# Folding w_phi into the key and query weights in blocks of six whole heads, with Wq transposed out of DRAM, Wv loaded in halves and a second order of the steps

## The chip, the cores and the metric

The kernel runs on one core of one Trainium2 chip. The metric is device time in microseconds (us) of one execution; three executions of the kernel before gave 236.93, 237.06 and 239.13 us, so the median is 237.06 us. Below, TensorE is PE, VectorE is DVE, ScalarE is ACT, GpSimd is POOL, and SyncE, which here only issues DMAs, is SP.

## The reference

There are 2048 tokens of 640 numbers in bf16, 32 heads of 20, and a second layer of 1728 hidden units.

```
qkv  = layernorm(x) @ wqkv                     # (2048, 3*640): q, k, v
pq   = einsum("bhsd,hdf->bhsf", q, w_phi)      # w_phi: (32, 20, 20), one small matrix per head
pk   = einsum("bhsd,hdf->bhsf", k, w_phi)
phi_q = concat(softmax(pq), softmax(-pq))      # 40 features per head
phi_k = concat(softmax(pk), softmax(-pk))
kv   = einsum("bhsf,bhsd->bhfd", phi_k, v);  z = sum over s of phi_k
o    = (phi_q @ kv) / (phi_q @ z + 1e-6)
h    = x + o @ wo
out  = h + silu(layernorm(h) @ w1) @ w2
```

## The kernel before

**Folding.** q and k are used only through w_phi. So the kernel multiplies the weights first: Wfk = Wk @ blockdiag(w_phi) and Wfq = Wq @ blockdiag(w_phi), both 640 x 640, and projects the tokens with these. PE contracts over partitions, so Wk and Wq have to be transposed to be the stationary operand. A row chunk `ce` holds 128 of the 640 input rows; there are C = 5 of them.

- Wk is loaded in five chunks (L168) and each is transposed on PE in five 128 x 128 pieces (`wk0` to `wk4`, L306), copied out of PSUM by DVE or ACT (`wke`, L323) into WTk, folded (`fk`, six matmuls into a pair of banks, L333) and copied into Wfk (`fk0e` and so on, L342).
- Wq is loaded whole (800 KB, L180). When it has landed, five SBUF-to-SBUF DMA transposes (`wq0` to `wq4`, L325) write WTq; `fq` and `fq0e` fold it as `fk` does.
- The pieces of 128 columns cut through heads (128 is not a multiple of 20). Each piece is therefore multiplied with a slab `phi` of 240 columns that overlaps its neighbours, and the overlaps are summed in PSUM: per chunk six matmuls of 80, 140 and 240 columns, 920 in all. `phi` is built by DVE out of w_phi and a 0/1 mask `own` (`phi_a`, `phi_b`, L292); POOL makes the mask.

**Tokens.** They are in T = 16 tiles of 128. For each tile t of X: `st` (L373, L374: mean and variance, DVE), `rs` (1/std, ACT or POOL), `xn` (normalised tile, L389, DVE 0.4 us or POOL 2.5 us), `xt` (transpose; on PE for the first four tiles, L396, by a DMA for the others, L418), `x` (copy into XnT for the first four, L416). Then `K` and `V` (ten matmuls of 320 columns each, L429), `ex` (exponentials, ACT, L461), `su` (sums, DVE, L465), `rk` (ACT), `sc` (scaling, DVE, L478), `ve` (values to SBUF, ACT, L482) and `kv` (eleven matmuls of 63 columns or fewer that add to the key-value matrix in PSUM banks 6 and 7, L497). The queries (`Q`, `qe`, `qs`, `qr`, `qt`), attention (`D`, `E`), the output projection (`G`, `ga`), the second layernorm (`ls`, `lr`, `hn`, `ht`) and the second layer (`u`, `s`, `lt`, `d`, `oa`, `out`) follow, overlapping.

**What sets the order.** Everything after the first loads is emitted by hand: ORDER is one list of step names, and each engine runs its own steps in the order of that list. ON says which engine does a step that several could do. The weights and X are loaded from SP's queue before the list starts: X tile 0, the five chunks of Wk, X tile 1, all of Wv, X tiles 2 and 3, all of Wq, X tiles 4 to 7, X tiles 8 to 15. The steps `load0` to `load11` bring wo, w1 and w2 later. `warm0` to `warm21` are matmuls on constants.

**Banks.** PSUM banks 0 to 5 are three pairs handed out in turn (`ps_pair`): a step that takes a pair waits until whoever read its previous content is done. Through the K and V stage each `wk` pair, `xt`, `fk`, `fq`, `K` and `V` takes the next pair; V of tile 0 alone is put into banks 6 and 7. There are four EK buffers and four VP buffers.

Of the kernel before, what the change touches and what calls it, by code (L numbers as in the profile page):

```python
# [30 lines left out]
ex15 su14 load8 Q2 ve14 qr1 rk14 V15 su15 qe2 qt1 Q3 sc12 ve15 sc13 rk15 Q4 qe3 sc14 sc15 kv12 qe4
kv13 qs2 kv14 kv15 Q5 qr2 Q6 qe5 bd1 qt2 bd0 Q7 qe6 qs3 qe7 halves D0 Q8 E00 E01 D1 qe8 qs4 Q9 ot0
load9 E10 Q10 qe9 load10 E11 Q11 qr3 qe10 qt3 D2 qe11 G00 E20 G01 ga00 ot1 Q12 ga01 E21 ls0 Q13 ot2
qe12 lr0 Q14 qe13 hn0 ht0 G10 qe14 D3 ga10 G11 load11 Q15 ga11 E30 E31 G20 qe15 ls1 u0.L ot3 u0.0
s0.L ga20 lr1 lt0 u0.4 s0.0 hn1 qr4 G21 ht1 s0.4 u0.8 ga21 ls2 u0.12 s0.8 G30 s0.12 lr2 G31 ga30 d00
hn2 ga31 ht2 ls3 qt4 u1.L qs5 lr3 u1.0 s1.L d01 hn3 s1.0 oa00 ht3 qr5 lt1 u1.4 oa01 qs6 qt5 u1.8
s1.4 qr6 u1.12 s1.8 out0 u2.L D4 s1.12 u2.0 qs7 s2.L lt2 d10 s2.0 qs8 qt6 E40 u2.2 E41 d11 s2.2 oa10
ot4 qr7 D5 oa11 u2.4 qs9 u2.6 s2.4 E50 u2.8 s2.6 E51 ot5 u2.10 s2.8 u2.12 qt7 s2.10 D6 s2.12 G40 E60
G41 E61 d20 ga40 ot6 ga41 ls4 out1 lr4 hn4 ht4 G50 G51 d21 ga50 oa20 ga51 ls5 d30 lr5 hn5 d31 qr8
ht5 oa21 oa30 G60 oa31 G61 ga60 qs10 D7 u4.L u4.0 s4.L lt4 E70 u4.2 s4.0 ga61 E71 u4.4 s4.2 qr9 ot7  # L40
u4.6 s4.4 ls6 qt8 u4.8 s4.6 lr6 out2 u4.10 qt9 s4.8 hn6 qr10 u4.12 s4.10 qt10 s4.12 out3 ht6 G70 G71
ga70 d40 ga71 ls7 lr7 D8 oa40 d41 E80 hn7 qs11 ht7 d50 E81 qr11 d51 oa41 qt11 oa50 qs12 u6.L u6.0
ot8 s6.L oa51 u6.2 s6.0 lt6 D9 s6.2 out4 u6.4 E90 E91 u6.6 s6.4 qr12 ot9 u6.8 s6.6 qs13 qt12 G80
s6.8 u6.10 u6.12 s6.10 D10 s6.12 G81 E100 G90 ga80 ga81 d60 ga90 ls8 E101 G91 lr8 d61 ot10 hn8 oa60
ga91 out5 ls9 ht8 d70 qr13 lr9 hn9 d71 oa61 ht9 out6 qt13 G100 G101 ga100 oa70 D11 oa71 u8.L u8.0
ga101 s8.L E110 u8.2 E111 s8.0 qs14 ot11 u8.4 s8.2 lt8 u8.6 qr14 s8.4 u8.8 ls10 qt14 s8.6 u8.10 lr10
s8.8 out7 hn10 u8.12 s8.10 qs15 ht10 s8.12 G110 G111 ga110 D12 d80 E120 ga111 E121 d81 ls11 ot12
oa80 lr11 d90 hn11 oa81 ht11 qr15 d91 oa90 G120 G121 ga120 oa91 u10.L D13 s10.L u10.0 lt10 E130 E131
u10.2 s10.0 ga121 ot13 ls12 u10.4 s10.2 lr12 u10.6 s10.4 hn12 u10.8 s10.6 ht12 u10.10 s10.8 out8
out9 qt15 u10.12 s10.10 D14 s10.12 G130 G131 ga130 d100 ga131 ls13 E140 lr13 d101 hn13 oa100 ht13  # L50
d110 oa101 E141 ot14 d111 oa110 out10 u12.L u12.0 s12.L D15 s12.0 u12.2 E150 oa111 G140 s12.2 E151
u12.4 ga140 ot15 u12.6 s12.4 out11 lt12 G141 s12.6 u12.8 ga141 ls14 u12.10 s12.8 lr14 G150 s12.10
hn14 u12.12 ga150 ht14 G151 s12.12 d120 ga151 ls15 lr15 d121 oa120 hn15 ht15 d130 oa121 out12 u14.L
oa130 u14.0 s14.L lt14 u14.2 s14.0 u14.4 s14.2 u14.6 s14.4 u14.8 s14.6 u14.10 s14.8 u14.12 s14.10
d131 s14.12 d140 oa131 out13 d141 oa140 d150 oa141 out14 d151 oa150 out150 d152 oa151 out151 oa152
out152
# [4 lines left out]
def kernel(  # L61
# [70 lines left out]
    def ps_half_bf16():  # L132
# [13 lines left out]
        phi_b="DVE", rs0="ACT", phi_a="DVE", xn0="DVE", wke0="ACT", wke1="ACT", wke2="DVE", wke3="ACT",  # L146
        x0="DVE", fk1e="ACT", fk2e="ACT", wke4="DVE", rs1="POOL", fk3e="DVE", fk4e="ACT", xn1="DVE",
        fk0e="ACT", rs2="ACT", x1="ACT", xn2="DVE", rs3="ACT", xn3="DVE", x2="DVE", rs4="POOL", xn4="DVE",
        rs5="POOL", xn5="POOL", x3="ACT", fq0e="ACT", rs6="POOL", fq1e="ACT", rs7="ACT", xn6="DVE", xn7="POOL",
        rs8="ACT", xn8="POOL", rs9="ACT", xn9="POOL", fq2e="ACT", fq3e="ACT", rs10="ACT", xn10="POOL",  # L150
        fq4e="ACT", rs11="POOL", xn11="POOL", rs12="ACT", rs13="POOL", xn12="DVE", xn13="POOL", rs14="ACT",
        xn14="POOL", rs15="ACT", xn15="POOL",
    )


    Wk = early.tile([P, C, D], BF16, name="Wk")
    Wq = early.tile([P, C, D], BF16, name="Wq")
    WPH = early.tile([P, C, DH], BF16, name="WPH")
# [8 lines left out]
    def load_wk(queue, a, b):  # L167
        queue.dma_start(Wk[:, a:b], wqkv_v[:, a:b, D : 2 * D])  # L168

    nc.scalar.dma_start(WPH[:], A_w_phi.rearrange("h d f -> (h d) f").rearrange("(r p) f -> p r f", p=P))  # L170
    load_x(0, 1)
    load_wk(nc.sync, 0, 1)
    load_wk(nc.sync, 1, 2)
    load_wk(nc.sync, 2, 3)
    load_wk(nc.sync, 3, 4)
    load_wk(nc.sync, 4, 5)
    load_x(1, 2)
    nc.sync.dma_start(Wv[:], wqkv_v[:, :, 2 * D : 3 * D])  # L178
    load_x(2, 4)
    nc.sync.dma_start(Wq[:], wqkv_v[:, :, 0:D])  # L180
    load_x(4, 8)
    load_x(8, 16)
# [25 lines left out]
    NV = 4  # L208
# [33 lines left out]
    def ones(i):  # L242
        nc.gpsimd.memset(VP[i][:, :, DH:HV], 1.0)
        nc.gpsimd.memset(EK[i][:, H * HF :], 0.0)

    assert NV == NE
# [14 lines left out]
    for side in range(2):  # L261
# [20 lines left out]
    nc.gpsimd.affine_select(
        out=own[:], in_=own[:], compare_op=ALU.is_ge, fill=0.0,
        base=DH - 1, pattern=[[-8, NB], [DH, 8]], channel_multiplier=-1,
    )
    nc.gpsimd.memset(phi[:, :, 8 * DH : BW], 0.0)
    ps_of = {}

    def phi_own(b):

        a, n = 3 * b, 3 - b
        engines[on(f"phi_{'ab'[b]}", "DVE")].tensor_tensor(  # L292
            phi[:, a : a + n, 0 : 8 * DH].rearrange("p r (h f) -> p r h f", f=DH),
            WPH[:, a : a + n].unsqueeze(2).to_broadcast([P, n, 8, DH]),
            own[:, a : a + n].unsqueeze(3).to_broadcast([P, n, 8, DH]), op=ALU.mult,
        )
# [5 lines left out]
    WTq = early.tile([P, C, NB, P], BF16, name="WTq")  # L302

    def transposed(W, ce, pt):
        for r in range(NB):
            nc.tensor.transpose(pt[:, r, :], W[:, ce, r * P : (r + 1) * P], ident[:])  # L306

    def wk(k, ce):
        if k == 4:

            pt = kv_bf[:, 1]
        else:
            if k % 2 == 0:
                ps_of["wk", "pair", k // 2] = ps_pair_bf16()
            pt = ps_of["wk", "pair", k // 2][:, k % 2]
        ps_of["wk", ce] = pt
        transposed(Wk, ce, pt)

    WKS = (0, 1, 2, 3, 4)
    for k, ce in enumerate(WKS):  # L320
        eng = on(f"wke{ce}", ("ACT", "DVE")[k % 2])
        add(f"wk{ce}", lambda k=k, ce=ce: wk(k, ce))
        add(f"wke{ce}", lambda ce=ce, e=copies[eng]: e(WTk[:, ce], ps_of.pop(("wk", ce))[:, 0:NB]))  # L323
    for ce in range(C):
# [523 lines left out]
```

## Time and profile before

| what | value |
|---|---|
| median of three executions | 237.06 us |
| span of the profiled execution, first to last instruction | 235.7 us |
| granted TensorE clock over the span | 1.000 |
| PE busy | 230.5 us, 98% |
| DVE / ACT / POOL busy | 170.0 / 107.8 / 46.7 us |
| PE busy from 30 to 200 us | 170.0 of 170.0 us |
| ten matmuls of 320 columns (a K or a V), start to start | 1.36 us |
| five 128 x 128 transposes on PE, start to start | 0.28 us |
| six matmuls of one fold, start to start | 0.40 us |
| eleven matmuls of one kv step, start to start | 0.34 us |
| copy of 640 columns out of PSUM, one instruction | ACT 0.69 us, DVE 0.44 to 0.49 us from bf16, 0.81 us from float32 |
| Wk chunk, issue to landing | 2.6 to 3.9 us |
| Wq, 800 KB, issue to landing | 8.3 us |
| X tiles 8 to 15, 1280 KB, issue to landing | 13.4 us |
| DMA transpose into XnT, issue to landing | 2.4 to 6.7 us, median 3.3 us |

The span is less than the measured time by 1.36 us against the median. A time read on one engine is turned into an effect on the end only where that engine, or whoever waits for it, has nothing else to do meanwhile. Durations of neighbouring instructions on one engine overlap by about 0.1 us (PE's by 0.16 us), so start-to-start distances are used for sums.

### The profile page before, as it was taken

The page shows a single profiled execution, that of the slowest core. Times are in us where ns is not written, and L with a number is a line of the kernel's source. Part 1 is how long each engine was busy: PE and PEld are TensorE (multiplying, and loading weights), DVE is VectorE, ACT ScalarE, POOL GpSimd, SP SyncE. Part 2 cuts the span into 40 slices and gives each one's busy share as a digit, 9 for nine tenths or more (in the row PEclk, how much of TensorE's full clock was granted, in tenths as well). Part 3 has the DMA queues.
Part 4 walks back from the last instruction along what each step waited for, and adds up shares of the span by engine and source line. Part 5 has one row for each costly group of instructions (what it writes and reads, how often), then busy time and mean ns, then how long its engine had stood idle before and what let it go on. Part 6 is the DMA issues. An engine that isn't in the chain of part 4 may idle for free.

```text
span 235.7 us, 5600 instructions
## 1 busy us (share of the span) xinstructions
PE 230.5 (98%) x2256; PEld 181.4 (77%) x2256; DVE 170.0 (72%) x355; ACT 107.8 (46%) x230; POOL 46.7 (20%) x80
## 2 busy tenths in 40 slices
PE   8899999999999999999999999999999999999995
PEld 6677777777777779798877878877877977877874
DVE  4699999899999758899669787696885544463021
ACT  3788997997888777231401501400510420421500
POOL 3117778990000011200020110011001100010000
PEclk9999999999999999999999999999999999999999
DMA  6996858499452842864431695617445193222001
GB/s 167 328 389 129 103 141 170 128 202 281 101 108 64 209 88 52 107 143 92 89 86 28 139 165 116 123 32 136 85 108 55 33 147 83 31 61 61 3 29 56
DMA packets 66697, 27.50 MB, mean 117 GB/s; under 512 B 58992, under 2 KB 65648, under 8 KB 66544
## 3 DMA queue, kind: packets, MB, share of 16 engines
q1 hardware_dynamic: 66016, 27.13, 53.2%
q8 instruction: 17, 0.28, 0.5%
q10 hardware_dynamic: 656, 0.03, 0.2%
q14 instruction: 8, 0.07, 0.1%
HBM read 10.43 MB, written 2.62 MB: 55 GB/s over the span
## 4 chain that ended last, share of the span: by engine, by line
PE 90%; DMA 6%; SPq 2%; issue 0%; DVE 0%; DVEq 0%
PE banks L733 24%; PE banks L771 24%; PE banks L429 15%; PE banks L444 9%; PE banks L643 9%; DMA Wq<-in_A_wqkv_dram 4%; DMA WTq<-Wq 3%; PE banks L497 2%; PE banks L610 2%; PE banks L774 2%; PE banks L744 1%; PE banks L333 1%; SPq L168 1%; SPq L165 1%; SPq L178 0%
## 5 line engine op out<-in xcount | busy, mean ns | idle before, releaser
L771 PE MATMUL banks<-w_sb,shT 128*128 128x320 bf16 (+2 forms) x429 | 61.3, 295 | 0.0
L733 PE MATMUL banks<-HnT,w_sb 128*128 128x256 bf16 (+1 forms) x585 | 60.0, 261 | 0.0
L733 PEld LDWEIGHTS <-w_sb 128*128 128x128 bf16 x585 | 51.3, 98 | 5.4
L771 PEld LDWEIGHTS <-shT 128*128 128x128 bf16 x429 | 41.1, 98 | 15.0
L753 ACT ACTIVATE shT<-banks 128x512 bf16<-128x512 f32 (+2 forms) x57 | 31.4, 559 | 36.0 <-PE banks L733 34.6
L429 PEld LDWEIGHTS <-XnT 128*128 128x128 bf16 x320 | 30.3, 98 | 12.0 <-issue 1.1
L382 POOL TENSOR_SCALAR rs<-mv 128x1 f32<-128x1 f32 x22 | 5.0, 227 | 159.9 <-DVE mv L374 159.8
L373 DVE BATCH_NORM_STATS2 st<-X 128x6 f32<-128x320 bf16 x64 | 27.9, 477 | 4.6 <-DMA X<-in_A_x_dram 4.5
L759 ACT ACTIVATE sh_l<-banks 128x128 bf16<-128x128 f32 x9 | 2.5, 278 | 62.4 <-PE banks L744 50.8
L780 DVE TENSOR_TENSOR o_t<-banks,X 128x320 bf16<-128x320 f32 (+2 forms) x33 | 15.5, 476 | 19.2 <-PE banks L774 19.2
L650 DVE TENSOR_TENSOR X<-banks,X 128x320 bf16<-128x320 f32 x32 | 15.3, 484 | 15.2 <-PE banks L643 15.0
L643 PE MATMUL banks<-wo_sb,OT 128*128 128x320 bf16 x160 | 25.1, 299 | 0.0
L429 PE MATMUL banks<-Wv,XnT 128*128 128x320 bf16 x160 | 23.8, 299 | 1.0 <-DMA Wv<-in_A_wqkv_dram 1.0
L557 ACT ACTIVATE EQ<-banks 128x660 bf16<-128x660 f32 (+2 forms) x48 | 21.8, 541 | 5.2 <-PE banks L444 5.0
L561 DVE TENSOR_REDUCE Sq<-EQ 128x66 f32<-128x1320 bf16 x16 | 24.2, 1516 | 0.0
L429 PE MATMUL banks<-Wfk,XnT 128*128 128x320 bf16 x160 | 24.0, 299 | 0.0
L444 PE MATMUL banks<-Wfq,XnT 128*128 128x360 bf16 (+2 forms) x160 | 23.3, 300 | 0.0
L465 DVE TENSOR_REDUCE Sk<-EK 128x64 f32<-128x1280 bf16 x16 | 23.3, 1465 | 0.0
L389 POOL TENSOR_SCALAR xn<-X,mv,rs 128x640 bf16<-128x640 bf16 x9 | 22.6, 2508 | 3.3 <-ACT rs L380 3.0
L461 ACT ACTIVATE EK<-banks 128x640 bf16<-128x640 f32 x32 | 20.7, 699 | 1.5 <-PE banks L429 1.4
L444 PEld LDWEIGHTS <-XnT 128*128 128x128 bf16 x160 | 15.4, 97 | 6.4
L643 PEld LDWEIGHTS <-OT 128*128 128x128 bf16 x160 | 15.2, 98 | 5.1
(63 smaller groups left out, 208.3 us busy)
## 6 DMA issues: line engine op xcount, KB each, us to landing
out_dram<-o_t SPq DMA_DIRECT2D x15, 160.0 KB, 2.1
w_sb<-in_B_w_dram SPq DMA_DIRECT2D x5, 432.0 KB, 4.4
w_sb<-in_B_w_dram SPq DMA_DIRECT2D x3, 480.0 KB, 6.4
X<-in_A_x_dram SPq DMA_DIRECT2D x1, 1280.0 KB, 13.4
Wk<-in_A_wqkv_dram SPq DMA_DIRECT2D x5, 160.0 KB, 3.8
Wv<-in_A_wqkv_dram SPq DMA_DIRECT2D x1, 800.0 KB, 6.5
Wq<-in_A_wqkv_dram SPq DMA_DIRECT2D x1, 800.0 KB, 8.3
wo_sb<-in_A_wo_dram SPq DMA_DIRECT2D x1, 800.0 KB, 5.0
```

Source lines behind the costliest of these rows:

```text
L373: nc.vector.bn_stats(st[:, i, :], X[:, t, i * HD : (i + 1) * HD])
L389: eng.tensor_scalar(out=xn_[t][:], in0=X[:, t, :], scalar1=mv_.pop(t)[:, 0:1], scalar2=rs_.pop(t)[:], op0=ALU.subtract, op1=ALU.mult,)
L429: nc.tensor.matmul(ps[:, g, 0:HD], XnT[:, c, t * P : (t + 1) * P], W[:, c, g * HD : (g + 1) * HD], start=(c == 0), stop=(c == C - 1),)
L444: nc.tensor.matmul(ps[:, 0 : e - a], XnT[:, c, t * P : (t + 1) * P], Wfq[:, c, a:e], start=(c == 0), stop=(c == C - 1),)
L461: nc.scalar.activation(E5[:, :, :, b, :], p4, AF.Exp, scale=sign)
L465: nc.vector.tensor_reduce(sk[t][:], ek[t][:, 0 : H * HF].rearrange("p (q f) -> p q f", f=DH), axis=AX.X, op=ALU.add)
L557: nc.scalar.activation(features(t, a, b)[:, :, :, i], p4, AF.Exp, scale=sign)
L561: nc.vector.tensor_reduce(sq[t][:], EQ[0][:, t, :, 0:FCH].rearrange("p c (q f) -> p c q f", f=DH), axis=AX.X, op=ALU.add)
L643: nc.tensor.matmul(ps[:, 0:HD], ot[t][:, c, :], wo_sb[:, c, g * HD : (g + 1) * HD], start=(c == 0), stop=(c == C - 1),)
L733: nc.tensor.matmul(ps[:, at : at + n], w1_sb[:, c, fc * P : fc * P + P], HnT[u][:, c, 0:n], start=(c == 0), stop=(c == C - 1),)
L753: nc.scalar.activation(shT[u][:, f0 * n : f1 * n], ps_of.pop(("u", u, f0))[:, 0 : (f1 - f0) * n], AF.Silu)
L771: nc.tensor.matmul(ps[:, 0 : b - a], shT[u][:, at : at + P], w2_sb[:, fc, a:b], start=(fc == 0), stop=False,)
```

## The change

- w_phi is folded in NB = 6 blocks: five of six whole heads (BW = 120 columns) and one of two heads (40 columns). No block cuts through a head, so nothing overlaps: every block is one matmul. The last block reads the last 128 columns of the weights, with zeros in `phi` for what is not its own.
- For the keys, `wk` makes six transposes per chunk in place of five, and WTk is 768 columns wide per chunk. `fk` is six matmuls of 120, ..., 120 and 40 columns.
- For the queries, Wq is no longer loaded. Six DMA transposes (`wq0` to `wq5`) read 640 rows x 128 columns of wqkv straight from DRAM into WTq. A fold `fq` is now one block for all five chunks: five matmuls of 120 (or 40) columns.
- Wv is loaded in two halves of 320 columns (`WV0`, `WV1`), and V of tiles 0 and 1 is cut into two steps each, one per half. Loads of X, Wk and Wv are steps of the list too: X0, the five Wk, WV0, X1, WV1, X2, X4, then `wq0`, `wq2`, then X8, `wq3`.
- `st1`, `xn0`, `xt0` and `x0` are cut in two steps; `xt` of the first four tiles writes into bank 6 or 7 and no longer takes a pair; V of tile 0 takes a pair.
- Eight VP buffers; w_phi comes in two DMAs; POOL builds the mask with four selects and clears all of `phi`.
- A new ORDER and a new ON. The list is changed all the way to the last two tiles. Its beginning is shown.

```diff
+warm0 warm1 warm2 warm3 warm4 warm5 warm6 warm7 warm8 warm9 warm10 warm11 warm12 warm13 warm14 warm15
+warm16 warm17 warm18 warm19 warm20 warm21 X0 WK0 WK1 st0 rs0 wk0 wk1 WK2 phi_b WK3 WK4 wk4 wke0 wke1 WV0
+phi_a wk2 wk3 wke4 fk0 xn0a X1 wke3 st1a wke2 WV1 ones4 xn0b xt0a st1b X2 fk0e ones7 ones0 ones3 rs1 X4
+x0a wq0 fk4 fk2 xt0b x0b xn1 fk1 fk4e st2 fk2e V0.0 fk1e st3 mask fk3 rs2 xt1 xn2 rs3 st5 fk3e wq2 x1
+V0.1 K0 ve0 st7 ex0 K1 xn3 X8 ones1 xt2 x2 V1.0 ones2 ones5 V1.1 rs5 ex1 rs7 st4 wq3 K2 xt3 ve1 rs4 x3
+su0 V2 xn4 st6 ex2 K3 ve2 ex3 V3 xt4 xn5 rs6 su2 rk0 pad1 ve3 st9 xn6 fq3 xt5 fq3e sc0 V4 fq0 ve4 kv0
+su1 xn7 K4 wq4 su3 rk2 V5 fq0e st8 rk1 rs9 ex4 sc1 wq1 xt6 st10 K5 ve5 rs8 kv1 sc2 ex5 xn9 xn8 fq1 fq1e
...
+qe2 sc13 qt1 Q4 rk15 ve15 qs2 qe4 Q3 Q5 load10 qe3 sc14 kv12 qt0 kv13 sc15 kv14 kv15 Q6 qr2 Q7 bd0 qe5
+bd1 qe6 halves D0 Q8 qs3 qt2 pad0 load7 qe7 D1 E00 Q9 E01 qe8 qe9 ot0 Q10 qr3 Q11 E10 qe10 E11 qs4 qe11
+D2 G00 ot1 G01 E20 G10 ga00 qt3 ga01 ls0 lr0 ga10 Q12 E21 load2 qe12 Q13 D3 qe13 qs6 hn0 G11 ga11 Q14
+ot2 E30 E31 Q15 ht0 qe14 qr4 ls1 qe15 G20 G21 u0.L ga21 ga20 s0.L u0.0 lr1 s0.0 hn1 ls2 ot3 ht1 u0.8
+u0.12 lr2 s0.12 qr6 lt0 qs5 G30 ga30 load11 G31 u0.4 ga31 ls3 hn2 s0.4 qr5 qt4 lr3 u1.0 s0.8 u1.12 ht2
...
+    NB = 6
+    BH = 6
+    BW = BH * DH
+    LB = D - (NB - 1) * BW
...
-    nc.scalar.dma_start(WPH[:], A_w_phi.rearrange("h d f -> (h d) f").rearrange("(r p) f -> p r f", p=P))
-    load_x(0, 1)
...
-    nc.sync.dma_start(Wv[:], wqkv_v[:, :, 2 * D : 3 * D])
-    load_x(2, 4)
-    nc.sync.dma_start(Wq[:], wqkv_v[:, :, 0:D])
-    load_x(4, 8)
-    load_x(8, 16)
+    def load_wv(g):
+        nc.sync.dma_start(
+            Wv[:, :, g * HD : (g + 1) * HD], wqkv_v[:, :, 2 * D + g * HD : 2 * D + (g + 1) * HD]
+        )
...
-    NV = 4
+    NV = 8
...
+        if b == 0:
+            o, w, m = phi[0:BW, 0 : NB - 1], WPH[0:BW, 0 : NB - 1], own[0:BW, 0]
+            n = NB - 1
+            nc.vector.tensor_tensor(
+                o.rearrange("p r (h f) -> p r h f", f=DH),
+                w.unsqueeze(2).to_broadcast([BW, n, BH, DH]),
+                m.unsqueeze(1).unsqueeze(3).to_broadcast([BW, n, BH, DH]), op=ALU.mult,
+            )
...
+    WTq = early.tile([P, NB, D], BF16, name="WTq")
+
+    def block_at(r):
+        return min(BW * r, D - P)
+
+    def load_transposed(WT, first, r):
+        at = first + block_at(r)
+        nc.sync.dma_start_transpose(WT[:, r : r + 1, :], A_wqkv[:, at : at + P])
+
+    def width(r):
+        return min(BW, D - BW * r)
+
+    def fold_block(WT, key, r):
+
+        w = width(r)
+        flat = ps_pair().rearrange("p b e -> p (b e)")
+        at = 512 - 4 * w
+        ps_of[key, r] = flat[:, at : at + C * w].rearrange("p (c f) -> p c f", f=w)
+        for ce in range(C):
+            nc.tensor.matmul(
+                ps_of[key, r][:, ce], WT[:, r, ce * P : (ce + 1) * P], phi[:, r, 0:w],
+                start=True, stop=True,
+            )
...
-        add(f"wq{ce}", lambda ce=ce: nc.sync.dma_start_transpose(WTq[:, ce], Wq[:, ce, :]))
...
+    def fold_rows(ce):
+
+        flat = ps_pair().rearrange("p b e -> p (b e)")
+        at = 512 - 3 * BW
+        ps = ps_of["fk", ce] = flat[:, at : at + D]
+        for r in range(NB):
+            nc.tensor.matmul(
+                ps[:, BW * r : BW * r + width(r)], WTk[:, ce, r, :], phi[:, r, 0 : width(r)],
+                start=True, stop=True,
+            )
...
+    def xn_transpose(t, a=0, b=C):
+        if a == 0:
+            ps_of["xn", t] = kv_bf[:, t % 2]
...
-        ps = ps_of[key, t] = kv_ps if (key, t) == ("V", 0) else ps_pair()
-        for g in range(2):
+        if 0 in gs:
+            ps_of[key, t] = ps_pair()
+        ps = ps_of[key, t]
+        for g in gs:
```

## The prediction

> **What bounds the kernel now.** I read the page first (busy time, slices), then the chain of waits, then PE's timeline, and only then DVE, ACT and SP over the first 40 us.
>
> ```profile
> PE 230.5 (98%) x2256; PEld 181.4 (77%) x2256; DVE 170.0 (72%) x355; ACT 107.8 (46%) x230; POOL 46.7 (20%) x80
> PE   8899999999999999999999999999999999999995
> ...
> PE 90%; DMA 6%; SPq 2%; issue 0%; DVE 0%; DVEq 0%
> ```
>
> PE is the bound, and full, up to the last slice. Only its first two slices (12 us) and single gaps can give anything back, besides PE work itself. The chain of waits (start, us, what) names one thing ahead of PE:
>
> ```profile
> 5.11 8.33 DMA Wq<-in_A_wqkv_dram
> 13.46 6.84 DMA WTq<-Wq
> 20.30 0.05 issue
> 20.35 0.57 PE banks L333 x6
> 20.92 1.36 PE banks L429 x10
> ```
>
> Those 15.2 us are not 15.2 us to win: PE works beside them. PE's timeline (start, busy us, in brackets the idle time before) shows what it lost:
>
> ```profile
> 0.83 4.36 PE L231 MATMUL banks<-const-bfloat16-1.0 128*128 128x256 bf16 x20 [0.83 <-PEq L832]
> 5.02 0.44 PE L306 MATMUL banks<-ident,Wk 128*128 128x128 bf16 x5
> ...
> 7.66 1.97 PE L333 MATMUL banks<-phi,WTk 128*128 128x240 bf16 x24
> 10.63 1.52 PE L429 MATMUL banks<-Wv,XnT 128*128 128x320 bf16 x10 [1.01 <-DMA Wv<-in_A_wqkv_dram]
> ...
> 12.27 1.52 PE L429 MATMUL banks<-Wfk,XnT 128*128 128x320 bf16 x10
> 13.89 0.45 PE L396 MATMUL banks<-ident,xn 128*128 128x128 bf16 x5
> ...
> 18.54 1.52 PE L429 MATMUL banks<-Wfk,XnT 128*128 128x320 bf16 x10
> 20.35 0.57 PE L333 MATMUL banks<-phi,WTq 128*128 128x240 bf16 x6 [0.29 <-DMA WTq<-Wq]
> ```
>
> The dense stream starts with V0 at 10.63. A K or V takes 1.36 us start to start, so 12.27 + 1.36 = 13.63 and xt2 came 0.26 us late (xn2 ended at 13.84), and 18.54 + 1.36 = 19.90, so fq0 came 0.45 us late. From there PE has no idle time. The end moves by three things alone: the start of the stream, these 0.71 us, and work added or removed.
>
> **PE work.** A query fold was 0.40 us, five make 2.00. Bounds for a matmul of 120 columns are the kv rows (63 columns: 0.34 / 11 = 31 ns) and the transposes (128 columns: 0.28 / 5 = 56 ns); I take 52 ns, near the transposes, and 31 ns for 40 columns. Then 25 x 52 + 5 x 31 ns = 1.45 us: **-0.55**. Bounds: 0.93 (all at 31 ns) to 1.68 us (all at 56 ns), so -1.07 to -0.32.
>
> The Trainium skill, TensorE: Matmul & The Clock Gate, section "Wait — 56ns, not 53.3ns?", says that when the sequencer decodes in software it spends about 62 ns on each matmul, which would bound short ones and speaks against cutting the folds up: 30 x 62 ns = 1.86 us, a gain of only 0.14. The 31 ns of the kv rows contradict that for this kernel.
>
> The key folds shrink too, but lie ahead of the stream, all but one: the new list has fk3 behind V0.0, 5 x 52 + 31 ns = **+0.29**. The five further transposes of Wk (0.28 us) lie in PE's waiting time ahead of the stream, which the DVE and ACT chains below cover; uncovered they would cost those 0.28.
>
> **When the stream can start now.** V0.0 needs XnT of tile 0, the first half of Wv, and its bank pair, which fk4e has to empty first (ps_pair: wk takes three pairs, then fk0, fk4, fk2, fk1, V0).
>
> Loads. The last chunk of Wk is issued at 3.12 and lands by 6.9 (3.8 after issue), as before. X1 landed at about 7.3; between it and Wv's landing (10.6) lay 800 KB in 3.3 us, so with 400 KB of Wv ahead of it X1 lands at about 8.9. Wv's second half stays at 10.6, X2 at 11.3. X4 landed at 15.0; without Wq, which took from 11.3 to 13.4, it is 12.9.
>
> ACT, from these rows (start, us):
>
> ```profile
> 5.50 2.18 ACT L323 COPY WTk<-banks 128x640 bf16<-128x640 bf16 x3 [0.53 <-PE banks L306]
> 7.58 1.36 ACT L342 CAST Wfk<-banks 128x640 bf16<-128x640 f32 x2
> 9.66 1.29 ACT L342 CAST Wfk<-banks 128x640 bf16<-128x640 f32 x2 [0.72 <-PE banks L333]
> ```
>
> Two copies take 1.29: about 0.6 per copy start to start, so 0.7 for 768 columns and 0.3 for the two chunks of x0a. The transposes of wk4 end at 6.9 + 0.33 + 0.2 = 7.4; wke4 8.1, wke2 8.8, fk0e 9.4, x0a 9.7, fk4e 10.3.
>
> DVE: phi_a (600 columns; 480 took 0.65, so 0.8) and xn0a are over by 8.1, wke3 by 8.6. Then st1a stands ahead of xn0b in DVE's queue and waits for X1: 8.9 + 0.45 (one of L373) + 0.25 (xn0b) = 9.6; st1b 0.6, x0b 0.3: 10.5. So V0.0 starts at max(10.3, 10.5) = 10.5, against 10.63: **-0.13**. The wait of 1.01 us for Wv is gone, and x0b and fk4e are what is late in its place. Bounds: 10.2 (X1 not delayed, ACT 0.1 quicker) to 11.0 (X1 0.5 later still).
>
> **Is the stream then dense?** V0.0 to 11.2, fk3 11.5, xt1 (rs1 on POOL 0.8 after 10.2, xn1 to 11.4) 11.8, V0.1 12.5. K0 needs all of Wfk: ACT does fk2e to 10.9, fk1e 11.5, and fk3e from 11.7 to 12.3. K1 12.5 + 1.36 = 13.8 (x1 12.9, ve0 13.5). Then K, V and one or two transposes follow to V3's end at 22.6, fq3, and V4 at 22.85. V4 is the first that needs a DMA transpose: DVE works off xn2 to 14.0, st5, st7, st4 (1.0 each), su0 (1.4), xn4 0.4: 18.8; xt4 then needs 3.2, as before: 22.0, 0.85 us ahead. Bank handovers (0.6 per ve, 1.2 per ex on ACT) come 0.25 to 0.6 us ahead of need. So none waits; the 0.71 us are gone: **-0.71**, with what a single handover could cost (0.1 to 0.5) kept for the range.
>
> SP's queue: wq0 and wq2 are issued at 6.3 to 9, ahead of X8 (1.3 us each, the rows of L325), with nothing behind them that is needed before st9 at 21; wq3 stands ahead of xt4, but is issued long before xn4 is ready. X8 landed at 19.8 and was first read at 21.2; 800 KB fewer lie ahead of it.
>
> Later: DVE's work up to sc15 is the same within 0.1 us (one more wke, qs2 moved ahead; fk3e, x2 and two xn moved away). kv15 then ends some 2.7 us before D0 wants KVB, and qr2 1.0 + both block masks 1.2 fit. load2 (w1) now comes behind qt3 at about 80, lands 4.4 later, and u0.L comes near 89. G10 comes about 0.7 us behind its transpose. PE's work there is unchanged, so I cost the rest of the list at nothing, with PE's other steps as cover; where it is thin, G10 and u1.0, a loss is 0.5 to 1 each.
>
> **The sum.** -0.55 + 0.29 - 0.13 - 0.71 = -1.1, and 0.1 given back in handovers: -1.0. Span 235.7 - 1.0 = 234.7; the median lies 1.36 above the span: **236.1 us**.
>
> **Rivals.**
>
> *A. The clock.* The first 20 warm matmuls took 218 ns for 256 columns, while later 320 columns take 136: PE ran at half rate until about 5.0, after 4.2 us of work (the granted clock reads 1.00 there nevertheless). Before, PE was then busy without a gap to 9.6. Now all warms come first (to about 5.6), and until 10.5 PE has some 3.1 us of work in 4.9 us (30 + 5 transposes, four of the key folds). If the half rate returns, the stream's first 4.2 us yield half: +2.1, so 238.2. For it: sparse work; against: no gap is over about 1.1 us. The Trainium skill, TensorE: Matmul & The Clock Gate, section "Part 1: The HAM clock gate", asks for an idle window of about 3.4 us before the clock falls; no run here shows a fall. Chance 0.09.
>
> *B. Thin handovers.* Two or three of those above lose 0.3 to 1 each: 236.7 to 238. For it: ACT is busy 9.46 of 10 us from 40 to 50; against: PE was never idle after 20.6 under the same pressure. Chance 0.17.
>
> *C. Slower: the DRAM transposes clog the queue.* wq0, wq2 and wq3 stand ahead of xt4 in one queue. If each occupies the DMA engines for d us, xt4 lands no earlier than 12.9 + 2d + 3.2 (X8, 1280 KB at 0.41 MB per us) + d + 1.2 = 17.3 + 3d. Up to d = 1.85 it hides; at d = 3 V4 waits 3.5 us and the time is 239.6; at d = 4, 242.6. For it: no transpose out of DRAM is in the trace, and rows of 256 bytes are short. Against: SBUF transposes of the same size landed 2.4 after issue, 1.2 of which is the issue, so d is near 1. The Trainium skill, DMA: Bandwidth & Descriptors, sections Specifications and "Latency and other measured facts", wants 512 bytes for line rate but gives transposes with a gap between rows 261 GB/s: estimated 0.6 us each, so hidden. Chance 0.14.
>
> *D. Nothing is stalled and the front comes earlier than either chain says*, or a fold costs 31 ns a matmul: 10.2 and -1.07 give 234.8 to 235.3; more only if landings are quicker. Chance 0.08.
>
> **How the numbers follow.** My own case (235.3 to 236.7) has 0.52. The range 235.0 to 238.2 takes in D in part, A and B; C and the rest of D are left out, 0.2 in all. 1% is 2.4 us, about what a measurement of this kernel can tell from no change: faster means under 234.7, which only part of D reaches: 0.06. Slower means over 239.4: C and, rarely, a pile-up in B: 0.16. Within: 0.78.
>
> **What would show it.** V0.0 starting at 10.2 to 10.9; no idle time on PE ahead of fq3 and V4; five matmuls of a query fold in about 0.26 us; Wfk's last copy ending just ahead of K0. A stream that starts after 11.2, a gap of PE at V4, or matmuls of 270 ns for 320 columns after 10 us would make it wrong.

## The result, and the profile after

| | kernel before | changed kernel |
|---|---|---|
| median | 237.49 us (22 executions, 236.79 to 239.13) | 238.43 us (22 executions, 237.63 to 238.83) |
| ratio to before, 95% interval | 1 | 1.0032 [1.0018, 1.0045] |
| span of the profiled execution | 235.7 us | 236.4 us |
| granted TensorE clock | 1.000 | 0.997 (1.00 up to 235.0 us, 0.50 for the 1.4 us behind, in which PE does nothing) |

The changed kernel is slower by 0.3% (0.94 us by the medians), less than the 1% taken here as the least that a measurement can tell from no change, but its interval excludes both no change and the gain of 1 us that was predicted. The prediction had 236.1 us and a range that ended at 238.2. Two medians of before stand in this document: 237.06 us of the three executions that the prediction started from, 237.49 us of the longer series beside the changed kernel; what is compared from here on is spans, and ratios on one chip. In the series of the experiments 6 of 35, 7 of 35 and 11 of 23 executions of the kernel before ran at a granted clock of 0.986 to 0.993 and took 238.9 to 241.5 us, which makes the ratios to it too low, so the table of the experiments has a second ratio, of the medians of the executions with a clock of 0.997 or more.

The page of the changed kernel, its busy line and slices of PE and its shares of the chain:

```profile
PE 230.3 (97%) x2261; PEld 181.6 (77%) x2261; DVE 168.3 (71%) x353; ACT 105.9 (45%) x227; POOL 55.7 (24%) x94
...
PE   8799999999999999999999999999999999999993
...
PE 93%; DMA 4%; SPq 1%; ACT 1%; issue 0%; DVE 0%; DVEq 0%
```

PE is as full as before. The loads of Wq and its transposes are gone from the chain. That the span grew by 0.7 us with PE's busy time lower by 0.2 us says that the difference lies in time without PE work, in a few short gaps, which an average over slices of 5.9 us hardly shows. Four points of both traces bracket them (us from the start of the span; K0 is the first matmul on Wfk, D0 the first that reads the finished key-value matrix):

| point | before | after | the stretch up to it, after less before (unrounded times) | predicted |
|---|---|---|---|---|
| K0 starts | 12.27 | 13.01 | +0.74 | +0.23 |
| D0 starts | 74.03 | 73.54 | -1.23 | -1.26 |
| PE's last matmul ends | 232.73 | 232.79 | +0.55 | 0 |
| span ends | 235.65 | 236.39 | +0.67 | 0 |

The second row is the change's own gain, and it came: PE's timeline of the changed kernel (start, busy us, operation) from the fourth K on; the view ends at 25 us, so its last row shows two of the eleven matmuls of a kv step.

```profile
20.36 1.52 PE L484 MATMUL banks<-Wfk,XnT 128*128 128x320 bf16 x10
21.72 1.52 PE L484 MATMUL banks<-Wv,XnT 128*128 128x320 bf16 x10
23.08 0.43 PE L329 MATMUL banks<-phi,WTq 128*128 128x120 bf16 x5
23.34 1.52 PE L484 MATMUL banks<-Wv,XnT 128*128 128x320 bf16 x10
24.70 0.43 PE L329 MATMUL banks<-phi,WTq 128*128 128x120 bf16 x5
24.96 0.23 PE L552 MATMUL banks<-VP,EK 128*128 128x63 bf16 x2
```

No row has a bracket with idle time. A query fold takes 0.26 us from start to start (23.08 to 23.34; 0.40 before), and V4 at 23.34 waits for nothing.

The three other rows are losses. **The front**, in the chain of waits of the changed kernel (start, us, what):

```profile
3.30 4.04 DMA Wk<-in_A_wqkv_dram
...
7.38 1.19 PE banks L343 x18
...
8.62 0.68 ACT WTk L359
...
9.31 0.71 ACT Wfk L362
10.03 0.29 ACT XnT L435
...
10.35 0.33 PE banks L420 x3
10.68 0.28 PE banks L351 x6
10.96 0.83 PE banks L484 x5
11.79 0.28 PE banks L351 x6
12.07 0.43 PE banks L420 x5
12.50 3.40 PE banks L484 x25
```

In this execution the last chunk of Wk landed at 7.34, not 6.9, and everything on ACT, which takes that chunk first, is later by the same 0.44 us: V0.0 starts at 10.95 instead of 10.5, K0 at 13.01 instead of 12.5. Whether that is the whole of it was to be tried.

**u0.L**, the first matmuls of the second layer, in the chain of waits of the changed kernel between 84 and 92 us:

```profile
85.29 0.70 PE banks L702 x5
85.99 0.01 issue
86.00 4.40 DMA HnT<-xn
90.40 0.05 issue
90.45 0.47 PE banks L803 x10
```

PE was ready at 89.91 and started at 90.45. The transposing load `ht0` is issued 0.20 us later than before (85.80 there), but landed 4.4 us after issue instead of 2.4. The single DMA records point to a load on the queue that the profile calls "instruction". The transpose reports its landing in 16 parts, and behind its data come 32 packets of 4 bytes, two for each part.

```
changed kernel:  ht0 issued 86.00; 15 of its 16 parts landed by 88.35, the last at 90.40
                 its packets of 4 bytes: 30 from 87.85 to 88.00, the last two at 89.29 and 89.30
                 instruction queue (q8), one load of 16 KB: 88.01 to 89.30
kernel before:   ht0 issued 85.80; all 16 parts landed by 88.17
                 its packets of 4 bytes: all 32 from 87.65 to 87.80
                 instruction queue (q8), one load of 16 KB: 89.30 to 90.63
```

The last two packets come in the moment in which the instruction load ends. The records don't name the DMA engine of a packet; that both were on the same one is read from these times.

**The tail.** The chain's last pieces, first of the changed kernel, then of the kernel before:

```profile
232.74 0.07 PE banks L833
232.81 0.03 issue
232.84 0.02 DVEq L839
232.86 0.40 issue
233.25 0.29 DVE o_t L839
```

```profile
232.68 0.07 PE banks L774
232.75 0.03 issue
232.77 0.02 DVEq L780
232.79 0.04 issue
232.84 0.29 DVE o_t L780
```

Both have the same five pieces, but ahead of DVE's last instruction, the addition for the last 128 columns, "issue" (time in which the engine waited for nothing that the profile shows) is 0.40 us instead of 0.04. In the DMA view of the last 3.4 us of the changed kernel there is a line that the same view of before does not have:

```profile
q14 instruction: 1, 0.01, 1.0%
```

It is one load of 8 KB from 233.93 to 234.50. One part of the last store is late beside it: 15 parts are complete at 235.03, the sixteenth at 235.47; before, both numbers are 234.60 and 234.61. DVE has 462 records before, and the last load of 8 KB of instructions in the span is at 226.32, after record 448. In the changed kernel DVE has 452 records (eight of the ten that are missing are waits with a record of their own), and the load comes after record 449: three from the end. The 0.40 us lie ahead of the load and not behind it, and the kernel before has them too, ahead of the record with the same number, at a place where DVE goes on to wait for PE:

```
kernel before:   DVE begins no record from 225.26 to 225.66, then record 448 of 462; load of 8 KB at 226.32
changed kernel:  DVE begins no record from 232.86 to 233.25, then record 448 of 452; load of 8 KB at 233.93
```

Record 448 of the changed kernel is the last addition; in the kernel before it is a wait for PE that ends at 227.04.

### The profile page after: what moved, and what is told of

It is laid out like the page before. It is cut to its first block, busy times and chain, and to the rows that moved or that the text cites. A ratio compares the mean times of both kernels' runs of the same rounds, so it can differ in the third digit from the quotient of the medians.

```text
span 236.4 us, 5600 instructions
## 1 busy us (share of the span) xinstructions
PE 230.3 (97%) x2261; PEld 181.6 (77%) x2261; DVE 168.3 (71%) x353; ACT 105.9 (45%) x227; POOL 55.7 (24%) x94
## 4 chain that ended last, share of the span: by engine, by line
PE 93%; DMA 4%; SPq 1%; ACT 1%; issue 0%; DVE 0%; DVEq 0%
PE banks L792 24%; PE banks L830 24%; PE banks L484 18%; PE banks L702 9%; PE banks L499 8%; PE banks L552 2%; PE banks L669 2%; DMA HnT<-xn 2%; PE banks L833 2%; DMA Wk<-in_A_wqkv_dram 2%; PE banks L803 1%; SPq L171 1%; PE banks L329 1%; PE banks L420 1%; PE banks L343 1%
## 5 line engine op out<-in xcount | busy, mean ns | idle before, releaser
L812 ACT ACTIVATE shT<-banks 128x512 bf16<-128x512 f32 (+2 forms) x57 | 30.1, 561 | 88.4 <-PE banks L792 67.8
L792 PE MATMUL banks<-HnT,w_sb 128*128 128x256 bf16 (+1 forms) x585 | 60.8, 261 | 0.0
L402 POOL TENSOR_SCALAR rs<-mv 128x1 f32<-128x1 f32 x25 | 6.6, 263 | 153.8 <-DVE mv L394 133.0
L410 POOL TENSOR_SCALAR xn<-X,mv,rs 128x640 bf16<-128x640 bf16 x11 | 27.6, 2515 | 0.2
L709 DVE TENSOR_TENSOR X<-banks,X 128x320 bf16<-128x320 f32 x32 | 14.9, 483 | 11.1 <-PE banks L702 10.7
L682 DVE TENSOR_TENSOR O<-banks,Rd 128x360 bf16<-128x360 f32 (+1 forms) x32 | 15.7, 491 | 1.5 <-DMA OT<-O 0.4
```

The lines of the kernel that those rows point to most:

```text
L410: eng.tensor_scalar(out=xn_[t][:, a * P : b * P], in0=X[:, t, a * P : b * P], scalar1=mv_[t][:, 0:1], scalar2=rs_[t][:], op0=ALU.subtract, ...
L792: nc.tensor.matmul(ps[:, at : at + n], w1_sb[:, c, fc * P : fc * P + P], HnT[u][:, c, 0:n], start=(c == 0), stop=(c == C - 1),)
L812: nc.scalar.activation(shT[u][:, f0 * n : f1 * n], ps_of.pop(("u", u, f0))[:, 0 : (f1 - f0) * n], AF.Silu)
```

## The experiments

Three theories, each for one of the losses: **F**, the front loses because ACT and PE take WK4, the chunk that lands last, ahead of two that landed before it; **H**, PE waits at u0.L because ht0 meets the instruction load on one DMA engine; **T**, the tail is longer because the shorter stream of DVE's instructions ends just behind a boundary of 8 KB. The rival to H and T was that these spots are chance, or that repairing one only uncovers the next wait. All runs in one table; "tail" is the distance from the end of PE's last matmul to the start of DVE's last instruction.

| kernel | ratio to before, 95% interval | ratio of medians, clock 0.997 or more | V0.0 | K0 | D0 | D0 to PE's end | tail |
|---|---|---|---|---|---|---|---|
| before | 1 | 1 | 10.63 | 12.27 | 74.03 | 158.70 | 0.11 |
| changed | 1.0032 [1.0018, 1.0045] | 1.0040 (all executions) | 10.95 | 13.01 | 73.54 | 159.25 | 0.46 |
| e1_dve12 | 0.9985 [0.9963, 1.0007] | 0.9995 | 10.44 | 12.98 | 73.90 | 159.21 | 0.11 |
| e2_hn0 | 0.9994 [0.9974, 1.0015] | 0.9998 | 10.42 | 13.07 | 73.99 | 158.70 | 0.48 |
| e3_warm16 | 1.0004 [0.9980, 1.0027] | 1.0012 | 10.70 | 13.16 | 73.67 | 158.71 | 0.46 |
| e4_arrival | 1.0012 [0.9987, 1.0036] | 1.0036 | 10.58 | 13.23 | 74.14 | 159.19 | 0.46 |
| e5_tail_hn0 | 0.9979 [0.9956, 1.0002] | 0.9999 | 11.26 | 13.37 | 74.28 | 158.72 | 0.10 |
| e6_ones6 | 0.9961 [0.9937, 0.9984] | 0.9976 | 10.51 | 13.04 | 73.57 | 158.71 | 0.11 |
| e7_v01 | 0.9950 [0.9918, 0.9981] | 0.9978 | 11.72 | 13.79 | 74.80 | 158.72 | 0.10 |
| e8_x1 | 0.9934 [0.9909, 0.9959] | 0.9955 | 10.58 | 12.64 | 73.16 | 158.72 | 0.11 |
| e9_x1_arrival | 0.9923 [0.9895, 0.9951] | 0.9951 | 9.85 | 12.21 | 72.96 | 158.72 | 0.10 |
| e10_x1_alone | 0.9982 [0.9951, 1.0012] | 1.0017 | 10.23 | 12.52 | 73.50 | 159.17 | 0.46 |

The last two columns take two values each, and which one a kernel has follows from its edits without exception. The ratios of single steps overlap; the trace columns carry the verdicts.

### e1_dve12: twelve instructions more on DVE

```diff
     NV = 8
+    spare = persist.tile([P, 1], F32, name="spare")
+    for _ in range(12):
+        nc.vector.memset(spare[:], 0.0)
```

> The changed kernel with 12 small memsets more on DVE at its start, where DVE waits until 3.3 us for X. In the profile of the changed kernel DVE starts its last instruction 0.40 us after PE's last matmul (0.04 before the change), with nothing to wait for, and an instruction fetch of 8 KB runs on one DMA engine from 233.9 to 234.5, so that the last store's sixteenth part lands at 235.47 and the fifteen others by 235.03. Theory T (the tail): DVE's instruction stream crosses from one 8 KB piece (128 instructions) into the next at its very end, since the change made it some ten instructions shorter; 12 more move the crossing ahead, the last instruction starts 0.04 us after PE, the store lands 0.4 us earlier, and the time falls by 0.6 to 0.8 us (ratio to the kernel before about 1.001, where the changed kernel has 1.0032 to 1.004). Rival: the tail is an accident of one execution, or the wait belongs to the store's own route: the time and the tail stay as they are within 0.15 us.

DVE's last load of instructions moved to 226.60, and the chain of waits ends as it does before the change:

```profile
233.15 0.02 DVEq L842
233.18 0.04 issue
233.22 0.29 DVE o_t L842
```

The last store is complete at 234.99 (15 parts at 234.95). Twelve instructions that compute nothing make the kernel quicker: T holds. The pause didn't go away, it lies elsewhere: DVE begins no record from 225.53 to 225.93, again ahead of record 448, of 464 now, and soon after it waits for PE as before. In each of the twelve profiles DVE pauses in this way for 0.40 us ahead of its record 448, and a load of 8 KB starts 0.65 to 0.95 us behind the pause. What DVE does in the pause no view shows. PE still waits at u0.L.

### e2_hn0 and e3_warm16: the load ahead of the collision, and the collision ahead of the load

```diff
-D2 G00 ot1 G01 E20 G10 ga00 qt3 ga01 ls0 lr0 ga10 Q12 E21 load2 qe12 Q13 D3 qe13 qs6 hn0 G11 ga11 Q14
+D2 G00 ot1 G01 E20 G10 ga00 qt3 ga01 ls0 lr0 ga10 Q12 E21 load2 qe12 Q13 D3 qe13 hn0 qs6 G11 ga11 Q14
```

> The changed kernel with hn0 put ahead of qs6 in DVE's queue, so that the transpose ht0 is issued about 0.5 us earlier. In the changed kernel PE waits 0.54 us for ht0 ahead of u0.L: 15 of the 16 parts of ht0 landed by 88.35, the last at 90.40, after an instruction fetch of PE (16 KB, 88.0 to 89.3) on that DMA engine. Theory H: PE runs 0.5 us ahead of the kernel before up to there and loses all of it in this one wait. With ht0 done before the fetch starts, u0.L starts at about 89.9 in place of 90.45, and PE's last matmul ends 0.5 us earlier; the time falls by 0.4 to 0.6 us. Rival: the next wait (ht1 at u1.0, or ot3 at G30) takes it, and PE's end moves by less than 0.15 us; or the last part is late again because the fetch is not what delayed it.

In e3 the list is untouched but for `warm16` to `warm21` at its start: PE runs six warm matmuls fewer, which puts its loads of instructions elsewhere in time:

```diff
-    WARM = 22
+    WARM = 16
```

> The changed kernel with 16 warm matmuls in place of 22: 12 instructions fewer on PE, so that each of PE's instruction fetches starts about 0.8 us of PE work later, the one near u0.L at 88.8 in place of 88.0, after all of ht0's data has moved (87.2 to 88.0). Nothing else is changed near u0.L. Theory H says that ht0 then lands about 2.4 us after its issue in all 16 parts and PE does not wait for it (u0.L at about 89.9, the time 0.4 to 0.6 us lower, less what the front loses or gains by a cooler or earlier start). Rival: ht0 is late for another reason (the queue, ot3 behind it), and u0.L waits as before. For the front: the half-rate phase would last longer, at most 0.5 us of PE work ahead of 10.9 us, where PE waits for loads anyhow.

Both lost the wait. What the tile HnT shows of ht0 in e2_hn0 (its landing after issue, us), then the chain of waits of e3_warm16 at the same place:

```profile
DMA to landing us min/median/max: 2.4/2.4/2.4
```

```profile
85.42 0.68 PE banks L702 x5
86.11 2.73 PE banks L499 x20
88.84 1.36 PE banks L702 x10
90.20 0.29 PE banks L803 x10
```

PE runs through to u0.L (L803). The instruction load in e2 comes at 88.30, when ht0's last packet is done (88.02; its last part is reported at 88.38); in e3 it comes at 89.04, with ht0's last packet at 88.13. In the four kernels that change neither (changed, e1, e4, e10) 15 parts are in by 88.3 to 89.0 and the sixteenth comes at 90.3 to 90.9, and its two packets of 4 bytes come within 0.02 us of the end of the instruction load. In the other eight kernels all 32 are done at least 0.1 us before the load starts. e3 is the sharper of the two, since it leaves ht0's place in the list alone and moves only the collision: H holds. D0 to PE's end falls by 0.55 us in both, to the value of before.

One piece stays open. The other 15 parts are reported 0.4 us after their packets; from 89.30 that would be 89.7, before PE was ready. The sixteenth took 1.1 us from there (1.1 to 1.2 in e1, e4 and e10), while the packets of the next transpose, ot3, ran. So the collision is shown to be needed for the loss, and how it grows from 89.30 to 90.40 is not.

### e4_arrival: the chunks of Wk in the order of their landing

```diff
-phi_a wk2 wk3 wke4 fk0 xn0a X1 wke3 st1a wke2 WV1 ones4 xn0b xt0a st1b X2 fk0e ones7 ones0 ones3 rs1 X4
+phi_a wke2 wk4 wke4 fk0 xn0a X1 wke3 st1a WV1 ones4 xn0b xt0a st1b X2 fk0e ones7 ones0 ones3 rs1 X4
```

(with `wk2 wk3` for `wk4` in the line above it, and fk2 ahead of fk4 and fk2e ahead of fk4e in the line below)

> The changed kernel with the chunks of Wk transposed and folded in the order in which they land (0, 1, 2, 3, 4 in place of 0, 1, 4, 2, 3; wke2 ahead of wke4 on ACT, fk2 ahead of fk4). In the changed kernel the chain is Wk chunk 4 landing at 7.34, 18 transposes to 8.6, wke2, fk0e and x0a on ACT to 10.0, xt0b, fk1, V0.0 at 10.95. Theory F: the front lost 0.45 us against the forecast because chunk 4 holds up the two that had landed, so that ACT starts its copies 0.7 us late; now ACT begins wke2 near 6.8, V0.0 starts at 10.2 to 10.5, K0 at 12.4 to 12.6, and PE runs 0.4 to 0.7 us ahead of the changed kernel up to u0.L. The time need not fall, since the wait for ht0 ahead of u0.L may take it. Rival: X1, xn0b and x0b on DVE set V0.0 (10.9 again), and nothing moves.

F is not the whole of it. ACT started its copies at 6.79 instead of 7.93, also because WK4 landed at 6.66 here, and V0.0 came 0.37 us earlier than in the changed kernel's profile, but no earlier than in e1, e2 and e6, which have the old order and WK4 by 6.9 (10.42 to 10.51). K0 came later, at 13.23. The chain of waits there doesn't pass through Wk at all:

```profile
4.26 4.99 DMA X<-in_A_x_dram
...
9.28 0.49 DVE st L392
...
10.49 0.22 DVE mv L394
...
11.10 0.58 POOL rs L405
...
11.70 0.51 DVE xn L410
```

It starts with X1, the second row tile; `xt1`, which stands between fk3 and V0.1 on PE, waits for the xn1 that ends here. It does so in e1, e2, e3 and e6 too (0.4 us each). There V0.0 starts at 10.4 to 10.7 and K0 still at 13.0 to 13.2. So two things hold K0 at 13: WK4 over ACT, and X1 over DVE and POOL. Repairing one shows the other.

### e5_tail_hn0 and e6_ones6: both repairs, and a fill moved forward

> The changed kernel with both repairs that each took its part back alone: twelve one-element fills on VectorE at the start (they only move the 8 KB boundary of its instruction stream away from its last stores) and hn0 ahead of qs6. If the two losses are separate, as my theory has it, they add: from the second KVB matmul group (D0) to TensorE's last matmul 158.6 to 158.8 us (159.25 in the changed kernel), VectorE's last instruction begins 0.1 us after TensorE ends (0.46), the last store's parts land together. The front is left as it is, with K0 at 13.0 and perhaps the wait of kv6 for ones6, so D0 at 73.5 to 74.0. Span 235.0 to 235.5, median 0.7 to 1.1 us below the kernel before's minus nothing else: ratio 0.995 to 0.998. Rival (one bound behind the other: a repaired loss only uncovers the next wait in the same stretch): the gain of the two together is no more than the larger alone, span 235.9 or above, ratio 0.998 to 1.0.

e5 has the edits of e1 and e2. Both losses are gone together (158.72 and 0.10): they add. The span is 235.8 and not 235.0 to 235.5, because in this execution PE could start on WK4 only at 7.70 (it waited 1.1 us) and because of a wait that the changed kernel's own profile does not have, in the waits of e5_tail_hn0 from 30 to 74 us:

```profile
PE banks L555 <- POOL VP L241: 0.3, 1, 0.3
```

This is kv6 waiting for the ones column of the seventh of the eight value buffers; the list places that fill (`ones6`) behind xn12 in POOL's queue, which is full from 15 to 50 us. The wait is there in e1, e2, e4, e5 and e10 and not in the changed kernel and e3; why POOL is 1 us later in some executions was not followed.

```diff
-phi_a wk2 wk3 wke4 fk0 xn0a X1 wke3 st1a wke2 WV1 ones4 xn0b xt0a st1b X2 fk0e ones7 ones0 ones3 rs1 X4
+phi_a wk2 wk3 wke4 fk0 xn0a X1 wke3 st1a wke2 WV1 ones4 xn0b xt0a st1b X2 fk0e ones7 ones6 ones0 ones3 rs1 X4
...
-xn12 su6 fq5e xt13 sc5 rk6 ones6 kv5 st14 sc6 ex8 ex9 rs15 su7 K10 rk7 su8 kv6 sc7 rs14 xt11 Q0 load4
+xn12 su6 fq5e xt13 sc5 rk6 kv5 st14 sc6 ex8 ex9 rs15 su7 K10 rk7 su8 kv6 sc7 rs14 xt11 Q0 load4
```

> As e5_tail_hn0, and the ones column of the seventh value buffer (ones6) is written early, behind ones7, instead of at 43 to 44 us behind xn12 in GpSimd's full queue. Theory: in the runs where kv6 waited for it (0.28 us of wait, 0.59 from start to start), D0 was 73.9 to 74.1 instead of 73.5; with the fill early, kv6 waits for nothing on GpSimd in any run and D0 comes at 73.4 to 73.6, another 0.3 to 0.4 us below e5_tail_hn0 if that one shows the wait, and nothing below it if it doesn't. Rival: kv6's real bound is GpSimd's stage work in the same queue (sc5, sc6, xn12), and the wait only changes its name: D0 stays at 73.9.

With the fill early (e6 to e9) kv6 waits in none of four executions. e6 has D0 at 73.57, with K0 at 13.04.

### e7_v01, e8_x1, e10_x1_alone and e9_x1_arrival: the front

In e7, V0.1 goes ahead of xt1 on PE; in e8, X1 is loaded ahead of the first half of Wv. Both have the edits of e6.

```diff
-x0a wq0 fk4 fk2 xt0b x0b xn1 fk1 fk4e st2 fk2e V0.0 fk1e st3 mask fk3 rs2 xt1 xn2 rs3 st5 fk3e wq2 x1
-V0.1 K0 ve0 st7 ex0 K1 xn3 X8 ones1 xt2 x2 V1.0 ones2 ones5 V1.1 rs5 ex1 rs7 st4 wq3 K2 xt3 ve1 rs4 x3
+x0a wq0 fk4 fk2 xt0b x0b xn1 fk1 fk4e st2 fk2e V0.0 fk1e st3 mask fk3 V0.1 rs2 xt1 xn2 rs3 st5 fk3e wq2 x1
+K0 ve0 st7 ex0 K1 xn3 X8 ones1 xt2 x2 V1.0 ones2 ones5 V1.1 rs5 ex1 rs7 st4 wq3 K2 xt3 ve1 rs4 x3
```

> As e6_ones6, and V0.1 stands before xt1 in TensorE's order. Theory of the front: K0's start is set by two things that end within 0.1 us of each other, TensorE's own dense work from V0.0 on (2.06 us from V0.0 to K0) and the chain from the second row tile's load over its moments to xt1 (xt1 at 12.05 to 12.26). With V0.1 in the place where xt1 waits, V0.0 at 10.4 gives fk3 11.1, V0.1 11.5, xt1 12.2, K0 12.5, as my prediction had K0: D0 0.4 to 0.5 us earlier than in e6_ones6, 73.0 to 73.1. Rival: the last casts of the folded Wk on ScalarE (fk3e ends at 12.8 in the changed kernel) or the row tiles behind bind next, and D0 moves by less than 0.15.

e7 can't be read: in its profiled execution one part of X1 landed at 10.39, 1.25 us after the fifteenth, with no instruction load beside it, and V0.0 itself came at 11.72. DVE's timeline of e7_v01 has the wait:

```profile
10.42 0.49 DVE L395 BATCH_NORM_STATS2 st<-X 128x6 f32<-128x320 bf16 x1 [1.63 <-DMA X<-in_A_x_dram]
```

xn0b, which V0.0 needs, stands behind st1a in DVE's queue, so a late X1 holds back tile 0 as well. The median is that of e6 (237.14 and 237.08).

```diff
-warm16 warm17 warm18 warm19 warm20 warm21 X0 WK0 WK1 st0 rs0 wk0 wk1 WK2 phi_b WK3 WK4 wk4 wke0 wke1 WV0
-phi_a wk2 wk3 wke4 fk0 xn0a X1 wke3 st1a wke2 WV1 ones4 xn0b xt0a st1b X2 fk0e ones7 ones6 ones0 ones3 rs1 X4
+warm16 warm17 warm18 warm19 warm20 warm21 X0 WK0 WK1 st0 rs0 wk0 wk1 WK2 phi_b WK3 WK4 wk4 wke0 wke1 X1 WV0
+phi_a wk2 wk3 wke4 fk0 xn0a wke3 st1a wke2 WV1 ones4 xn0b xt0a st1b X2 fk0e ones7 ones6 ones0 ones3 rs1 X4
```

> As e6_ones6, and the second row tile's load X1 is issued ahead of WV0 instead of behind it, PE's order unchanged. Theory of the front: X1 lands 0.5 to 1.0 us earlier (8.0 to 8.4 instead of 8.9 to 9.3), xn1 comes at 11.0 instead of 11.5, xt1 no longer waits, and K0 comes at V0.0 + 2.06: 12.5 if V0.0 begins at 10.4, D0 0.4 us earlier than in e6_ones6. Rival: WV0, then later by the same 0.5 us and more, makes V0.0 late instead (10.9 to 11.0), and D0 moves by less than 0.15; or VectorE, which takes st1 between its copies of the transposed Wk, shifts the queue there and xn0 with it.

X1 landed at 7.64, xt1 no longer waits, and K0 comes 2.06 us after V0.0, at 12.64; D0 is 0.41 us earlier than in e6. The chain of waits of e8_x1 is now that of WK4:

```profile
3.31 3.66 DMA Wk<-in_A_wqkv_dram
...
7.01 1.19 PE banks L346 x18
...
8.25 0.68 ACT WTk L362
...
8.94 0.71 ACT Wfk L365
```

> The changed kernel with the load X1 ahead of WV0 and nothing else. Theory: the front is a term of its own, so K0 at 12.5 to 12.8 (13.01) and D0 at 73.1 to 73.3 (73.54); the wait of u0.L for ht0 (0.4 to 0.7 us from start to start) and the 0.46 us between TensorE's end and VectorE's last instruction stay as they are, so that span and median fall by 0.3 to 0.5 us: ratio 1.000 to 1.003 of the kernel before. Rival (the front is slack against the wait of u0.L, whose instruction fetch and transposing load come at their own time): D0 earlier, but u0.L waits longer by the same and TensorE ends where it did, span 236.3 to 236.5.

In e10, which has this edit alone, K0 is at 12.52, as theory had it, and the span (236.3) is the rival's. But the 0.5 us did not go where the rival put it: u0.L lost 0.45 us, less than the 0.54 of the changed kernel. It went to kv6, which waited 0.3 us (0.59 from start to start) for ones6, so D0 came at 73.50.

> As e8_x1 (both repairs, ones6 early, X1 ahead of WV0), and the steps of the folded Wk in the order in which their loads land, as in e4_arrival, where the first copies began at 6.8 us instead of 7.9 and V0.0 didn't pay. Theory: in e8_x1 the chain to K0 no longer goes through X1 but through the last chunk WK4 (landing 6.96), its transposes, one copy, one cast, one copy of x0 and V0.0; with the landed chunks first, ScalarE starts its copies up to 1 us earlier, and now the gain is not swallowed by xt1: V0.0 at 10.1 to 10.4 instead of 10.58, K0 0.2 to 0.5 us earlier, ratio 0.0005 to 0.002 below e8_x1's. Rival: WK4 is now transposed last and its fold is last, so that the same chain closes one copy later: V0.0 within 0.15 us of e8_x1, no gain, or xt1 waits again and K0 stays at 12.6.

e9 is e8 with the edit of e4. With X1 early, the arrival order of Wk does pay at the front: V0.0 at 9.85, K0 at 12.21, 0.43 us earlier. D0 kept 0.20 of that; the rest was lost in small steps between 40 and 61 us, which were not followed, and the ratio can't be told from that of e8.

e8 and e9 are quicker than both kernels: their profiled spans are 234.7 and 234.5 us against 235.7 and 236.4, and e9 takes 0.9923 [0.9895, 0.9951] of the time before by the first ratio and 0.9951 by the second, which agrees with the spans (0.995).

## Why the prediction was wrong

The sum was -1.0 us against the kernel before, and the span came out at +0.7. By the steps of the prediction:

- **Query folds, -0.55, and the two waits at xt2 and fq0, -0.71: right.** From K0 to D0 the changed kernel is 1.23 us shorter, against 1.26. In part this is luck of the execution: in e1, e2, e4, e5 and e10, where kv6 waits for ones6, it is 0.78 to 0.85, and the prediction had that wait at nothing ("So none waits"). The kv rows as one bound and the transposes as the other held the fold well: 0.26 us.
- **DRAM transposes (rival C): fell.** They landed 3.7 to 8.6 us after issue (median 5.2) and held SP for 1.2 to 2.2 us each, more than the 1.2 taken; nothing on PE waited for them. **Clock (rival A): fell**; ten matmuls take 1.36 us from the first K on, and no row of 270 ns appears after 10 us.
- **V0.0 at 10.5: right where WK4 lands as taken.** In e1, e2 and e6, which leave the loads and the steps ahead of it as they are, it was 10.42 to 10.51; in the profile of the changed kernel 10.95, with WK4 at 7.34 instead of 6.9, and in e5, which leaves them too, 11.26 with WK4 at 7.65. The landing of WK4 lies between 6.66 and 7.65 in the eight profiles with this order of loads; why was not followed, and the prediction's bounds for V0.0 didn't ask for it.
- **"Is the stream then dense?": the step that failed at the front.** It put xn1's end at 11.4 and xt1 at 11.8. In e1, where X1 landed at 9.01, against the 8.9 taken, mv1 was done at 10.46 (10.2 taken), rs1 on POOL took 0.99 us with its handovers (0.8) and xn1 took 0.50 (0.4) and ended at 11.95: 0.55 us late in three short links, each mis-sized by 0.1 to 0.3 us. PE then waits at xt1, one step behind the V0.0 that the prediction had watched. With the late WK4 or without it, K0 comes at 13.0, and 0.5 us is lost.
- **"PE's work there is unchanged, so I cost the rest of the list at nothing": the step that failed at u0.L.** PE's work was unchanged and load2, which the prediction looked at, landed in time. It didn't ask when the other operand of u0.L lands. A load of 2.4 us after issue had 1.5 us in hand before; the new order left it as much by the issue (86.00 to 89.91), but put it beside an instruction load that held up its last part: +0.55.
- **The tail was no term of the sum.** It belongs to "the rest of the list", which was costed at nothing; its instructions are the same, and the prediction took that for the same time. Ten records fewer in all of DVE's stream put the pause ahead of record 448 on the last addition, and the load of 8 KB beside the last store: +0.35 on DVE and +0.32 behind it, +0.67 in the span. This is larger than the gain on the query folds.

So -1.0, with 0.5, 0.55 and 0.67 on top: +0.7. Rival B had the size of such losses (0.3 to 1 each) but looked for them at PSUM handovers on ACT, at G10 and at u1.0, where none came. (The lower end of rival D, 234.8, doesn't come out of its own two terms: 236.1 - 0.3 - 0.52 is 235.3.) The range took in the bounds of the costs that were named; the three terms that moved the sign were in none of them.

## What to carry to other kernels

When PE is full, what a change is worth is decided by the few places where a wait ends within half a microsecond of need; for each of them follow every operand back to its load, and not only the one that the change touches. Two kernels with the same work can differ by 0.3% through the length of an instruction stream alone: compare where each engine's instruction loads fall, above all near the end and beside transfers that are awaited, before a difference of this size is put down to the change. Repairs of separate losses add (e5); a repair that shows nothing (e4, e10) may sit ahead of a second wait at the same point or in the same stretch.

## What the runs showed of the hardware

- An instruction load can hold up one part of a data transfer. PE's come as 16 KB each, 17 in the span, about one per 256 records of PE (matmuls and weight loads together) and 0.9 to 1.5 us long in the two profiles; the others are of 8 KB and 0.3 to 0.8 us. A transfer that is reported in 16 parts is done when its last part is: 15 parts of ht0 at 88.35, one at 90.40. That one DMA engine carried the load and the late part is read from the times (89.30 for both), not from a record.
- DVE begins nothing for 0.40 us ahead of its record 448 in twelve profiles of twelve; in the kernel before it does so ahead of record 320 as well, 128 records earlier (153.97 to 154.37). In seven kernels DVE waits for PE right behind it and nothing is lost; in five record 448 is the last addition, which starts 0.35 to 0.38 us later for it. The Trainium skill, Runtime: NRT & Kernel Launch, section "Instruction fetch mechanics", says that instructions are streamed in blocks of 16 KiB by a DMA queue of each engine's own and that crossing a block costs little, mostly hidden. For PE the block size agrees with the 17 loads of 16 KB; the loads that go with DVE's pauses are of 8 KB. "Mostly hidden" agrees with most of the 25 instruction loads in the changed kernel's span, but two of them go with losses on the path, of 0.55 and 0.67 us.
- One part of a load can be late with no instruction load in sight: X1 in e7, 1.25 us behind the fifteenth part. Its cause stays open, as does POOL's delay of ones6 in some executions.
